# A weight's sign kept as a signed zero that POOL or VectorE makes, and a new fixed order of instructions

## The chip, the core and the metric

One core of a Trainium2 chip runs the whole program. The metric is the device time of one execution in microseconds (us). TensorE (PE in the profile) does the matrix products, VectorE (DVE), ScalarE (ACT) and GpSimd (POOL) the elementwise work, SyncE (SP) issues the DMAs.

## The reference

Attention in which a query sees only the keys of its own cluster, and behind it a feed-forward net with a softplus. The weights reach the device as 64-bit floats (a float32 draw times a float64 scale), all other inputs as float32.

```python
q_assign = argmax(einsum(q / |q|, c / |c|))          # 4 x 8 x 768 rows of 64, 16 clusters per head
k_assign = argmax(einsum(k / |k|, c / |c|))
scores = where(q_assign[..., None] == k_assign[..., None, :], q @ k.T / 8, -1e9)
attn = softmax(scores)
x = (attn @ v).transpose(0, 2, 1, 3).reshape(3072, 512)
h = x @ w_in                                          # w_in 512 x 2048
out = (maximum(h, 0) + log1p(exp(-abs(h)))) @ w_out   # w_out 2048 x 512
```

## The kernel before

Every product is made of three float16 products: an operand is split into a high part (a cast) and a low part (the operand minus that cast). There are 192 score tiles of 128 queries by 768 keys, numbered by `t`. For each one TensorE makes the scores into PSUM (line 1021), VectorE takes the negated row maximum `negm` from PSUM (line 1037), ScalarE the exponential (line 1048); the result is split (helpers `cast` at line 539 and `sub` at line 529), transposed by DMA or by TensorE, and multiplied with `v` into `mbank` (lines 1153 to 1159). The first net layer `h` (lines 1236 to 1238) and the second `o` (lines 1319 to 1321) of a stretch of 384 tokens follow among the score tiles of later stretches, so TensorE has products of three stages at once. Where the writer of the program saw a gap on TensorE early on, filler products are issued (line 494).

The order of the work is written out. Each step of each task is a generator that yields operations; the list `SEQUENCE` names them one after the other. An entry is 1000 x choice + task: the task's next operation is issued, and if it can run on several engines the choice says on which (0 the first one named). The planner's costs and biases that stand in the yields (660, 420, `SBIAS`) do not choose anything in this program; the list does. Each engine runs its instructions in the order of the list.

The change is in `prep_weights`. The two weights are loaded in 32 steps of 128 rows by 512 columns of 64-bit words, 16 for `w_in` and 16 for `w_out`, most of them into tiles that later hold other parts of `wo` (so the profile calls the loaded words `wo`, and two `wraw`). `low` and `high` are the two 32-bit words of each number, so reads and writes of them step over every second word. A step does this before: ScalarE makes the magnitude (`AF.Abs` of the high word, scaled, line 663); the low word is shifted right by 29, on VectorE (line 669) or by a scaled `Relu` on ScalarE (line 670); VectorE joins the sign bit of the high word with the shifted low word (line 678), and joins the magnitude, shifted left by 3, into that (line 684). Then `cast` and `sub` split it (lines 539 and 529). Step s+1 waits for the magnitude of step s, and a step from the third on waits for a score tile (`sc`, one per 1.2 steps), so the steps spread over the first 40 or so score tiles. `cast` can run on ScalarE, VectorE or POOL, `sub` on POOL or VectorE.

```python
yield op("ACT", 660, lambda: nc.scalar.activation(mag, val, AF.Abs, scale=sc))
od.set(("wd", step))
yield op(("DVE", "ACT"), (420, 770), (
    lambda: nc.vector.tensor_scalar(low, low, 29, None, ALU.logical_shift_right),
    lambda: nc.scalar.activation(low, top, AF.Relu, bias=down, scale=2.0**-13)), ...)
yield op("DVE", 685, lambda: nc.vector.scalar_tensor_tensor(
    high, high, -0x80000000, low, ALU.bitwise_and, ALU.bitwise_or), shared=True)
yield op("DVE", 685, lambda: nc.vector.scalar_tensor_tensor(
    high, mab, 3, high, ALU.logical_shift_left, ALU.bitwise_or), shared=True)
```

Of the kernel before, what the change touches and what calls it, by code (L numbers as in the profile page):

```python
# [9 lines left out]
F32 = mybir.dt.float32  # L10
I32 = mybir.dt.int32
I64 = mybir.dt.int64
U16 = mybir.dt.uint16
# [24 lines left out]
SLACK = 0  # L38
BIAS = 500
# [366 lines left out]
def tile_cluster_attention__then__softplus_ffn(  # L406
# [91 lines left out]
    def op(eng, ns, emit, **opt):  # L498
        return ("op", eng, ns, emit, opt)
# [915 lines left out]
```

## Time and profile before

| | |
|---|---|
| time, median of 3 runs | 825.93 us (825.83 to 826.98) |
| the profiled execution | 828.08 us, of which the span from the first to the last instruction is 826.3 us |
| TensorE busy | 809.5 us, 98% of the span |
| VectorE busy | 641.5 us, 78% |
| ScalarE busy | 566.6 us, 69% |
| POOL busy | 444.7 us, 54% |
| granted TensorE clock | 0.999 of full |

The shares of the whole span are averages over stages with different limits: up to 200 us VectorE and ScalarE are busy almost all the time, after that TensorE alone. The stage has to be chosen before a row is read, and POOL's and VectorE's rows have to be read together.

### The profile page before, as it was taken

The numbers are of one execution on the slowest core, as the hardware profiler recorded it, in microseconds if no ns is written. First come the engines' busy times: TensorE is split into PE (matmuls) and PEld (weight loads), VectorE is DVE, ScalarE is ACT, GpSimd is POOL, SyncE is SP. The second block draws the span as 40 slices with busy tenths as digits, with TensorE's granted clock in tenths as the row PEclk, the third lists the DMA queues.
The fourth block names the chain that finished last, engine by engine and source line by source line (L and its number), as shares of the span: only waits on it lengthen the run. The fifth ranks groups of instructions, "written<-read, shape, count | busy, mean of one in ns | idle before, by whom it ended". The sixth has DMA issues, their size and how long they took to land.

```text
span 826.3 us, 19518 instructions
## 1 busy us (share of the span) xinstructions
PE 809.5 (98%) x7904; PEld 518.4 (63%) x7904; DVE 641.5 (78%) x1142; ACT 566.6 (69%) x977; POOL 444.7 (54%) x353
## 2 busy tenths in 40 slices
PE   8999989999999999999999999999999999999998
PEld 8888866665666666656665656656666665555553
DVE  8999989998868887779795879878898776632432
ACT  7999998997867768666676658585567665443330
POOL 4226444646775746674567374766575755632220
PEclk9999999999999999999999999999999999999999
DMA  9436999999979999999989979999969966640001
GB/s 330 153 85 160 213 195 232 210 208 180 210 160 193 182 194 198 206 198 206 166 134 181 171 150 193 206 217 176 192 128 181 179 127 105 115 90 13 27 1 39
DMA packets 386315, 134.29 MB, mean 163 GB/s; under 512 B 362672, under 2 KB 379056, under 8 KB 386224
## 3 DMA queue, kind: packets, MB, share of 16 engines
q1 hardware_dynamic: 386224, 133.03, 80.8%
q8 instruction: 62, 1.02, 0.5%
q14 instruction: 29, 0.24, 0.1%
HBM read 35.68 MB, written 6.29 MB: 51 GB/s over the span
## 4 chain that ended last, share of the span: by engine, by line
PE 73%; DVE 9%; ACT 8%; DMA 6%; POOL 3%; issue 2%; SPq 0%; POOLq 0%; DVEq 0%; ACTq 0%
PE s L1021 10%; PE o L1319 9%; PE o L1321 9%; PE o L1320 9%; PE h L1236 8%; PE h L1238 8%; PE h L1237 8%; PE mbank L1159 3%; PE mbank L1157 3%; PE mbank L1158 3%; DMA pt<-phl 2%; DVE negm L1037 2%; ACT p L1048 2%; DVE wo L678 1%; DMA rawq<-in_q_dram 1%
## 5 line engine op out<-in xcount | busy, mean ns | idle before, releaser
L1048 ACT ACTIVATE p<-s,negm 128x768 f32<-128x768 f32 x190 | 170.5, 901 | 95.0 <-DVE negm L1037 77.2
L1037 DVE TENSOR_REDUCE negm<-s 128x1 f32<-128x768 f32 x192 | 181.2, 948 | 35.5 <-PE s L1021 35.0
L529 POOL TENSOR_TENSOR phl<-p,phl 128x768 f16<-128x768 f32 x87 | 148.8, 1717 | 71.3 <-ACT phl L539 45.8
L1236 PE MATMUL h<-xT,wi 128*128 128x384 f16 x512 | 166.7, 326 | 1.4 <-ACT fg L1275 0.5
L1238 PE MATMUL h<-xT,wi 128*128 128x384 f16 x512 | 166.8, 326 | 0.0
L1237 PE MATMUL h<-xT,wi 128*128 128x384 f16 x512 | 166.8, 326 | 0.0
L1021 PE MATMUL s<-kt,qt 128*128 128x384 f16 x768 | 155.8, 326 | 4.2 <-ACT p L1048 2.3
L1321 PE MATMUL o<-wo,gh 128*128 128x512 f16 x384 | 145.5, 379 | 0.0
L1320 PE MATMUL o<-wo,gh 128*128 128x512 f16 x384 | 145.5, 379 | 0.0
L1319 PE MATMUL o<-wo,gh 128*128 128x512 f16 x384 | 145.4, 379 | 0.0
L1285 POOL TENSOR_TENSOR fg<-fg,fa 128x384 f32<-128x384 f32 x63 | 67.4, 1072 | 93.3 <-ACT fa L1281 90.0
L1157 PE MATMUL mbank<-vb,pt 128*128 128x65 f16 x1008 | 108.9, 192 | 3.2 <-DVE fg L1285 1.6
L1158 PE MATMUL mbank<-vb,pt 128*128 128x64 f16 x1008 | 109.0, 192 | 0.0
L1159 PE MATMUL mbank<-vb,pt 128*128 128x65 f16 x1008 | 108.7, 194 | 0.0
L1157 PEld LDWEIGHTS <-pt 128*128 128x128 f16 x1008 | 93.7, 98 | 15.9 <-DMA pt<-phl 3.9
L1021 PEld LDWEIGHTS <-qt 128*128 128x128 f16 x768 | 71.4, 98 | 50.4 <-issue 5.8
L1158 PEld LDWEIGHTS <-pt 128*128 128x128 f16 x1008 | 93.0, 97 | 12.5 <-issue 0.6
L1159 PEld LDWEIGHTS <-pt 128*128 128x128 f16 x1008 | 93.2, 97 | 0.0
L539 ACT CAST phl<-p 128x768 f16<-128x768 f32 x97 | 79.6, 829 | 19.0 <-DMA pt<-phl 12.8
L529 DVE TENSOR_TENSOR phl<-p,phl 128x768 f16<-128x768 f32 x75 | 84.1, 1132 | 8.2 <-ACT phl L539 3.4
L1267 ACT ACTIVATE fa<-h 128x384 f32<-128x384 f32 x78 | 38.1, 489 | 66.5 <-PE h L1238 56.2
L529 POOL TENSOR_TENSOR gh<-fg,gh 128x768 f16<-128x768 f32 x35 | 58.7, 1676 | 25.1 <-ACT gh L539 20.6
(177 smaller groups left out, 1460.0 us busy)
## 6 DMA issues: line engine op xcount, KB each, us to landing
wo<-in_moe_w_in_dram SPq DMA_DIRECT2D x16, 512.0 KB, 6.3
wo<-in_moe_w_out_dram SPq DMA_DIRECT2D x14, 512.0 KB, 4.3
rawk<-in_k_dram SPq DMA_DIRECT2D x16, 384.0 KB, 4.8
rawq<-in_q_dram SPq DMA_DIRECT2D x16, 384.0 KB, 4.2
rawv<-in_v_dram SPq DMA_DIRECT2D x16, 384.0 KB, 4.2
out_dram<-ot SPq DMA_DIRECT2D x24, 256.0 KB, 2.4
pt<-phl SPq DMA_TRANSPOSE x82, 5.9
wraw<-in_moe_w_out_dram SPq DMA_DIRECT2D x2, 512.0 KB, 5.5
```

Of the source, the lines that this page charges most:

```text
L529: [lambda e=e: e.tensor_tensor(dst, a, b, ALU.subtract) for e in (nc.gpsimd, nc.vector)],
L1021: nc.tensor.matmul(st[:, j, :SH], qt[:, s, i], kt[:, s, NT // 2 * j : NT // 2 * (j + 1)], start=(s == 0), stop=(s == 1),)
L1037: yield op("DVE", 950, lambda: nc.vector.tensor_reduce(negm, st[:, :, :SH], AX.XY, ALU.max, negate=True))
L1157: nc.tensor.matmul(av, pt[:, 0, c], vb[:, c, D : 2 * D + 1], start=(c == 0), stop=False)
L1158: nc.tensor.matmul(av[:, :D], pt[:, 0, c], vb[:, c, :D], start=False, stop=False)
L1159: nc.tensor.matmul(av, pt[:, 1, c], vb[:, c, D : 2 * D + 1], start=False, stop=(c == NT - 1))
L1236: nc.tensor.matmul(hp, w[0], x[0], start=(c == 0), stop=False)
L1237: nc.tensor.matmul(hp, w[0], x[1], start=False, stop=False)
L1238: nc.tensor.matmul(hp, w[1], x[0], start=False, stop=(c == NP - 1))
L1319: nc.tensor.matmul(po, g[0], wo[:, f, 0, 0], start=(f == f0), stop=False)
L1320: nc.tensor.matmul(po, g[0], wo[:, f, 0, 1], start=False, stop=False)
L1321: nc.tensor.matmul(po, g[1], wo[:, f, 0, 0], start=False, stop=(f == f0 + NF // 2 - 1))
```

## The change

In a weight step the magnitude becomes `Copy` with a scale (its sign stays, and is shifted out later), which ScalarE, POOL or VectorE may do. The low word is no longer shifted by itself. The high word is multiplied by 0.0 in place, on VectorE or POOL, which leaves a zero with the number's sign; this operation writes what the magnitude reads, so it waits for it. The first join shifts the low word by 29 and joins it with that signed zero; the second is as before. So the step has as many operations as before. The constant `down` and its fill go. In `prep_k` the copy of the high part of a key becomes a `cast` with a choice of engine. The list is another one throughout, of the same length, 3654 entries.

```diff
-        yield op("ACT", 660, lambda: nc.scalar.activation(mag, val, AF.Abs, scale=sc))
+        yield op(
+            ("ACT", "POOL", "DVE"),
+            (686, 640, 420),
+            (
+                lambda: nc.scalar.activation(mag, val, AF.Copy, scale=sc),
+                lambda: nc.gpsimd.tensor_scalar(mag, val, sc, None, ALU.mult),
+                lambda: nc.vector.tensor_scalar(mag, val, sc, None, ALU.mult),
+            ),
+            shared=True,
+            bias=MBIAS,
+        )
         od.set(("wd", step))
         yield op(
-            ("DVE", "ACT"),
-            (420, 770),
-            (
-                lambda: nc.vector.tensor_scalar(low, low, 29, None, ALU.logical_shift_right),
-                lambda: nc.scalar.activation(low, top, AF.Relu, bias=down, scale=2.0**-13),
-            ),
+            ("DVE", "POOL"),
+            (420, 640),
+            [lambda e=e: e.tensor_scalar(val, val, 0.0, None, ALU.mult) for e in (nc.vector, nc.gpsimd)],
             shared=True,
             bias=SBIAS,
         )
         yield op(
             "DVE",
             685,
-            lambda: nc.vector.scalar_tensor_tensor(high, high, -0x80000000, low, ALU.bitwise_and, ALU.bitwise_or),
+            lambda: nc.vector.scalar_tensor_tensor(high, low, 29, high, ALU.logical_shift_right, ALU.bitwise_or),
             shared=True,
         )
...
-            yield op("ACT", 830, lambda: nc.scalar.copy(n2[:, :, :D], n1[:, :, D:]))
+            yield cast(n2[:, :, :D], n1[:, :, D:], NT * P)
```

What the two lists say, read by walking them through the generators: all 32 magnitudes stay on ScalarE, and so do the 12 key copies. The shifts of before stand 19 times on ScalarE and 13 times on VectorE; the multiplications by zero of after stand 18 times on POOL and 14 times on VectorE. TensorE's 969 operations come in the same order but for exchanges among neighbours: 457 keep their place, and none moves by more than 7. From behind the first row maximum (`t` = 0) up to and with the 49th (`t` = 48) these counts differ, among the operations that read and write SBUF alone:

| operation | before | after |
|---|---|---|
| shift, then multiplication by zero | POOL 0, ACT 17 | POOL 16, ACT 0, and one more on VectorE |
| weight `cast` | | 2 fewer on POOL, 2 more on ACT |
| weight `sub` | | 2 more on POOL, 1 fewer on VectorE |
| key `sub` | | 1 more on POOL, 1 fewer on VectorE |
| `cast` of `p` | | 1 more on POOL, 1 fewer on VectorE |
| `sub` of `p` | | 2 fewer on POOL, 2 more on VectorE |

## Rows read from the trace of the kernel before

**Rows 1.** The page: the span, busy time and share of each engine (part 1), and the busy tenths and granted clock in 40 slices of 20.7 us (part 2).

```profile
span 826.3 us, 19518 instructions
...
PE 809.5 (98%) x7904; PEld 518.4 (63%) x7904; DVE 641.5 (78%) x1142; ACT 566.6 (69%) x977; POOL 444.7 (54%) x353
...
DVE  8999989998868887779795879878898776632432
ACT  7999998997867768666676658585567665443330
...
PEclk9999999999999999999999999999999999999999
```

**Rows 2.** Windows: the length of a stretch, then busy us of each engine with the number of its instructions, granted clock, DMA share and GB/s. The first row lasts from the end of the first row maximum to the end of the 49th; the others follow it up to 780 us.

```profile
24.00:181.00 157.00, 148.75 (x1537) 114.75 (x1534) 151.65 (x280) 150.33 (x281) 73.60 (x61) 1.00 0.83 176
...
181.00:240.00 59.00, 58.14 (x583) 35.61 (x582) 47.76 (x87) 41.68 (x70) 37.13 (x27) 1.00 1.00 194
240.00:780.00 540.00, 539.13 (x5177) 327.39 (x5176) 406.75 (x667) 343.54 (x572) 319.11 (x242) 1.00 0.85 160
```

**Rows 3.** Groups of VectorE's instructions in the stretch from 24 to 181 us, by line and shape: count, busy us and mean ns of one, then idle time before them. First the row maximum, which reads PSUM; then those that read and write SBUF alone, down to groups of 0.9 us.

```profile
L1037 DVE TENSOR_REDUCE negm<-s 128x1 f32<-128x768 f32 x48 | 44.6, 945 | 0.8 <-PE s L1021 0.8
L678 DVE SCALAR_TENSOR_TENSOR wo<-wo 128x512 int32<-128x512 int32 x30 | 20.8, 694 | 0.7 <-ACT wo L663 0.3
L684 DVE SCALAR_TENSOR_TENSOR wo<-wi,wo 128x512 int32<-128x512 int32 x16 | 10.8, 679 | 0.0
L684 DVE SCALAR_TENSOR_TENSOR wo<-wo 128x512 int32<-128x512 int32 x14 | 10.3, 740 | 0.0
L529 DVE TENSOR_TENSOR phl<-p,phl 128x768 f16<-128x768 f32 x8 | 8.0, 1013 | 0.1
L669 DVE TENSOR_SCALAR wo<-wo 128x512 int32<-128x512 int32 x12 | 5.1, 422 | 0.0
L1285 DVE TENSOR_TENSOR fg<-fg,fa 128x384 f32<-128x384 f32 x9 | 5.0, 571 | 0.0
L529 DVE TENSOR_TENSOR gh<-fg,gh 128x768 f16<-128x768 f32 x4 | 4.1, 1034 | 0.0
...
L922 DVE SCALAR_TENSOR_TENSOR qn<-rawq,qn 128x768 f16<-128x768 f32 x3 | 2.8, 946 | 0.0
L529 DVE TENSOR_TENSOR wo<-wo 128x512 f16<-128x512 f32 x4 | 2.7, 686 | 1.6 <-POOL wo L539 1.6
L529 DVE TENSOR_TENSOR wi<-wo,wi 128x512 f16<-128x512 f32 x4 | 2.7, 681 | 0.0
L971 DVE TENSOR_SCALAR n<-n 128x96 f16<-128x96 f16 x3 | 2.4, 784 | 0.0
L529 DVE TENSOR_TENSOR vb<-rawv,vb 128x768 f16<-128x768 f32 x2 | 1.9, 952 | 0.0
...
L529 DVE TENSOR_TENSOR xn<-x,xn 128x384 f16<-128x384 f32 x2 | 1.1, 549 | 0.0
...
L922 DVE SCALAR_TENSOR_TENSOR qn<-rawq,qn 128x384 f16<-128x384 f32 x2 | 1.1, 542 | 0.0
...
L529 DVE TENSOR_TENSOR kn<-rawk,kn 128x768 f16<-128x768 f32 x1 | 0.9, 950 | 0.0
```

**Rows 4.** One line's instructions over the whole run: the least, the median and the greatest duration in ns, when the first and the last start. The row maximum; subtractions and casts on POOL and VectorE; VectorE's second join and its small product of line 971; POOL's product of line 977, which works on two sizes.

```profile
L1037 DVE TENSOR_REDUCE negm<-s x192: 915/947/959, 23.0 to 717.3; 128x1 f32<-128x768 f32 x192
...
L529 POOL TENSOR_TENSOR phl<-p,phl x87: 1631/1644/2450, 101.4 to 721.5; 128x768 f16<-128x768 f32 x87
L529 DVE TENSOR_TENSOR phl<-p,phl x75: 939/952/2384, 94.8 to 721.3; 128x768 f16<-128x768 f32 x75
...
L529 POOL TENSOR_TENSOR wi<-wo,wi x12: 1154/1168/1512, 34.3 to 79.7; 128x512 f16<-128x512 f32 x12
...
L529 POOL TENSOR_TENSOR kn<-rawk,kn x6: 1642/1742/2362, 116.2 to 501.2; 128x768 f16<-128x768 f32 x6
...
L539 POOL CAST phl<-p x33: 813/822/1635, 205.3 to 716.5; 128x768 f16<-128x768 f32 x33
...
L539 DVE CAST phl<-p x32: 540/550/1737, 175.1 to 720.8; 128x768 f16<-128x768 f32 x32
...
L539 POOL CAST wi<-wo x5: 647/654/1050, 29.4 to 81.1; 128x512 f16<-128x512 f32 x5
...
L684 DVE SCALAR_TENSOR_TENSOR wo<-wo x14: 676/684/1449, 84.7 to 176.8; 128x512 int32<-128x512 int32 x14
...
L971 DVE TENSOR_SCALAR n<-n x4: 180/759/835, 19.1 to 54.8; 128x96 f16<-128x96 f16 x4
...
L977 POOL TENSOR_TENSOR n<-qn,aq x18: 825/1468/2182, 19.1 to 658.5; 128x768 f16<-128x768 f16 x14, 128x384 f16<-128x384 f16 x4
```

**Rows 5.** The timeline (start and duration in us) around 176 us, one row of POOL's and one of VectorE's.

```profile
175.85 1.88 POOL L529 TENSOR_TENSOR phl<-p,phl 128x768 f16<-128x768 f32 x1 [5.01 <-ACT fg L1275]
...
176.83 1.45 DVE L684 SCALAR_TENSOR_TENSOR wo<-wo 128x512 int32<-128x512 int32 x1
```

**Rows 6.** ScalarE's shift of the low words from 24 to 181 us, as in rows 3.

```profile
L670 ACT ACTIVATE wo<-wo,down 128x512 int32<-128x512 uint16 x17 | 13.1, 780 | 0.0
```

**Rows 7.** Who released TensorE from its waits between 24 and 181 us: us in total, times, longest.

```profile
PE s L1021 <- ACT p L1048: 2.0, 5, 0.6
...
PE h L1236 <- ACT fg L1275: 0.5, 1, 0.5
```

More of the change, by code (lines that the diff above doesn't have):

```diff
@@ L38 @@
 SLACK = 0
+MBIAS = 500
 BIAS = 500
@@ L622, in tile_cluster_attention__then__softplus_ffn @@
     rooms = {}
-    down = cpool.tile([P, 1], F32, name="down")
-    nc.vector.memset(down, 2.0**-14 - 0.5)
     def prep_weights(step: int):
@@ L649, in prep_weights @@
         low, high = words[:, :, 0], words[:, :, 1]
-        top = raw64.bitcast(U16).rearrange("p (e t) -> p e t", t=4)[:, :, 1]
         val = high.bitcast(F32)
```

328 rows, old and new, of the table SEQUENCE are left out of this document.

## The prediction

> **What bounds the kernel now.** I read the page first. TensorE is busy 98% of the span at the full granted clock, so the whole can gain little; but VectorE's and ScalarE's slices show eights and nines for the first ten slices, some 200 us, and sixes and sevens after them [rows 1]. All 32 weight steps lie in that first part, so the windows are cut there. From the end of the first row maximum to the end of the 49th, 24 to 181 us, VectorE is busy 151.65 of 157.0 us, ScalarE 150.33, TensorE 148.75, POOL only 73.60. From 181 to 240 us TensorE has 58.14 of 59, and from 240 to 780 us 539.13 of 540 [rows 2]. So in the first part the elementwise engines set the pace, and behind it TensorE runs without gaps: what the first part gains or loses moves the end by as much, because TensorE has no room in which to make it up.
>
> On this reading POOL has 83 us free in the first part, and ScalarE's work could go there at no cost. Whether it can is seen in the durations. VectorE's row maximum, which reads PSUM, takes 915 to 959 ns in 192 cases, whatever POOL does. VectorE's instructions that work on SBUF alone have a median near their least and a far greater maximum: the subtraction 952 and 2384 ns, the small product of line 971 180 and 835; POOL's have the same tails (1644 and 2450, a cast 654 and 1050) [rows 4]. The timeline shows why: POOL's subtraction runs from 175.85 to 177.73 us, VectorE's join starts at 176.83 and lasts 1.45 us instead of its 0.684, so it does its work when POOL is through [rows 4, 5]. POOL and VectorE's SBUF work take turns.
>
> So the resource to add up is this turn: all of POOL's time plus VectorE's time on SBUF alone. VectorE's groups of that kind in the first part, added down the list from line 678 to the last row: 20.8 + 10.8 + 10.3 + 8.0 + 5.1 + 5.0 + 4.1 + 2.8 + 2.7 + 2.7 + 2.4 + 1.9 + 1.1 + 1.1 + 0.9 = 79.7 us [rows 3]. With POOL's 73.6 that is 153.3 of 157.0 us [rows 2]. Some of it is waiting, counted on both sides: on VectorE 14 x (740 - 684) + 8 x (1013 - 952) + 4 x (1034 - 952) + 3 x (784 - 180) ns = 3.4 us [rows 3, 4]. POOL's own waiting is in the sum too, and VectorE's groups under 0.9 us are not; I let these two cancel. That leaves 149.9 us of work in turn, and 7.1 us of room in 157. POOL looks half idle, yet the turn is 95% full.
>
> The Trainium skill has this as a rule: SBUF — State Buffer, section "SBUF: two separate sides", says that VectorE and GpSimd share a pair of SBUF ports by an exclusive lock held for the whole instruction, by VectorE's two-input and fast one-input SBUF operations, while ScalarE has ports of its own. By that rule the trace agrees (1449 ns for a join of 684 beside POOL), and the rule speaks against this change. Without it, POOL counted as free, the change would come out faster by the price in the first rival.
>
> **The change part by part.** ScalarE's shifts go: in the first part 17 of 0.780 us, 13.1 us [rows 6]. That is 9% of ScalarE's time there, and it used no turn. ScalarE takes two weight casts back.
>
> The multiplications by zero come. No row shows one. On VectorE I take the shift of the low words, 422 ns for the same 128 x 512 words with the same step [rows 3]; there is one more of them than there were shifts, +0.4 us. On POOL the nearest row is its cast of the same words, 654 ns: one input, same count, same step. The bounds are from nothing, if POOL did it in turns that nobody wants, to POOL's two-input subtraction on the same count, 1168 ns [rows 4]. I take 0.654, since it too reads one tensor. 16 of them in the first part: +10.5 us in turn.
>
> The new list moves other work [rows 3, 4]. Two weight casts leave POOL: -1.3. Two weight subtractions go onto POOL and one leaves VectorE: 2 x 1.168 - 0.681 = +1.7. One key subtraction goes from VectorE to POOL: 1.742 - 0.950 = +0.8. One cast of `p` does so: 0.822 - 0.550 = +0.3. Two subtractions of `p` go the other way: 2 x (0.952 - 1.644) = -1.4. The first join costs what it did, since it is the same instruction with two SBUF inputs; the second is untouched. The magnitude stays on ScalarE in all 32 steps, `Copy` for `Abs` with the same shape, so nothing. The key copies stay on ScalarE, nothing. The fill of `down` was one column before the first score tile, nothing.
>
> In sum the turn gets 10.5 + 0.4 - 1.3 + 1.7 + 0.8 + 0.3 - 1.4 = 11.0 us more in the first part, 160.9 us of work for 157.0 us. VectorE's own work does not change by 1 us, and it has 5.4 us idle in the stretch, so a POOL instruction that takes the turn mostly makes VectorE late, and with it the row maxima, the exponentials and TensorE.
>
> The new wait, the zero behind the magnitude, holds the joins of its step. In 19 steps the shift already followed the magnitude on the same engine, 0.78 us behind it, so the chain of a step grows in 13 steps only, by 0.42 to 0.65 us. Behind a waiting zero on VectorE stands the next row maximum in its list; on POOL a subtraction. No load is moved, and TensorE's list keeps its order but for exchanges of up to seven places, so no DMA queue is passed by anything else.
>
> If all the room were used up, the 49th row maximum would end 160.9 - 157.0 = 3.9 us later; if the room of before stays, because it comes from POOL lacking an operand and not from choice, 11.0 us later. Nearer the second: the room is small, VectorE leaves little, and the new pieces are short and each need a turn of their own. ScalarE's relief helps a little the other way. I let a third of the room go: 11.0 - 7.1 / 3 = 8.6 us.
>
> The profiled execution took 828.08 us, 826.3 of span and 1.8 around it; it lies 2.15 us above the median of 825.93. On its scale the forecast is 828.1 + 8.6 = 836.7, on that of the median 825.9 + 8.6 = 834.5 us.
>
> **The rivals.** Faster: ScalarE is the limit of the first part, and the room in the turn takes the zeros. For it speaks ScalarE's 150.33 of 157 [rows 2]. Then TensorE gets back what ScalarE's waits cost it, 2.0 + 0.5 us [rows 7], and the time is 823.4. It decides if the turn holds less than 146 us of work, since only then do 11.0 fit into 157. Against it stands the sum, 149.9. Chance 0.07.
>
> No change: POOL's zeros fall under VectorE's PSUM work, 44.6 us of row maxima and more, and ScalarE's gain pays for the rest. Against it: POOL's 73.6 us already have to fit into the 77 us that VectorE's 79.7 leave. 825.9 within 1.6. Chance 0.06.
>
> Dearer: POOL's multiplication costs what its two-input operations do, or the list, whose TensorE order was barely touched while the engines behind it run otherwise, opens gaps after 181 us where there were 1.7 us in 600 [rows 2]. The first is 16 x (1.168 - 0.654) = 8.2 us more, 842.7. Nothing in the rows speaks for it, and nothing excludes it. Chance 0.10.
>
> **How the numbers follow.** The forecast has 0.77. Its own range is 3.9 to 11.0 us, 829.8 to 836.9. To leave out no more than 2 in 10 the range goes to 829.0 below, short of both the faster and the unchanged case (0.13), and to 841.0 above, which takes in most of the dearer one. A measurement of this kernel can tell about 0.2% from no change, 1.6 us. Faster by more has 0.07; within it 0.06; slower 0.77 + 0.10 = 0.87.
>
> **What the profile of after would show.** If the steps are right: POOL busy up by some 10 us within the first 49 row maxima; ScalarE less than 90% busy there; VectorE still without idle time, its means on SBUF lines (678, 684 and 529 of before) further above their medians; the 49th row maximum ending at 185 to 192 us instead of 181; and from there to the end the same time as before. A zero on POOL at 0.64 to 0.70 us. I am wrong if the 49th row maximum ends at 181 or earlier with POOL that much busier, for then the turn was not full; or if the time is lost after 200 us, for then the new order and not the turn did it; or if the zeros take far from 0.65 us.

## The result, and the profile after

The changed kernel takes 832.62 us (median of 3 runs, 832.55 to 832.81) against 825.93 us (825.83 to 826.98): a ratio of 1.0078, 95% interval 1.0055 to 1.0101. It is slower, and 834.5 us had been forecast. The profiled execution took 832.81 us, of which the span is 831.0 us. It lies 0.2 us above the median of its kernel, while that of before lay 2.15 us above its own; so the medians differ by 6.7 us and the two traces by 4.7 us of span.

The page of the changed kernel, to be laid beside [rows 1]: span, busy time and share of each engine, and the tenths in 40 slices.

```profile
span 831.0 us, 19676 instructions
...
PE 814.4 (98%) x7992; PEld 523.7 (63%) x7992; DVE 653.6 (79%) x1126; ACT 558.5 (67%) x969; POOL 476.0 (57%) x376
...
DVE  8999999999887987889777878887587887743222
ACT  7998789977867668677476555786587565433530
...
PEclk9999999999999999999999999999999999999999
```

POOL has 31 us more and ScalarE 8 us less, as the change has it; but VectorE has 12 us more, and it was given 16 instructions fewer (1126 against 1142). Its nines now reach the tenth slice without a break, and the clock is full throughout. The windows say where the time went; the first lasts again from the end of the first row maximum to the end of the 49th, as in [rows 2]:

```profile
23.80:186.10 162.30, 154.28 (x1602) 119.36 (x1601) 158.31 (x280) 142.20 (x265) 101.30 (x77) 1.00 0.78 173
186.10:250.00 63.90, 63.17 (x646) 39.06 (x645) 57.59 (x97) 48.92 (x82) 35.52 (x28) 1.00 0.87 182
250.00:790.00 540.00, 539.01 (x5168) 327.52 (x5167) 406.25 (x649) 338.54 (x573) 321.66 (x251) 1.00 0.79 159
```

The first part took 162.3 instead of 157.0 us, and its end lies 5.1 us later. Behind it nothing more is lost: TensorE is busy 63.17 of 63.9 us and 539.01 of 540 us, as before. So the question is what made the first part 5.3 us longer. VectorE is busy 158.31 us in it instead of 151.65 (+6.7) and idle 4.0 instead of 5.35 (-1.4), which is the 5.3. VectorE's groups in that stretch, with count, busy us, mean ns of one, and idle time before them, answer to [rows 3]:

```profile
L1042 DVE TENSOR_REDUCE negm<-s 128x1 f32<-128x768 f32 x48 | 44.8, 947 | 0.0
L683 DVE SCALAR_TENSOR_TENSOR wo<-wo 128x512 int32<-128x512 int32 x30 | 24.0, 810 | 2.4 <-POOL wo L676 2.2
...
L530 DVE TENSOR_TENSOR phl<-p,phl 128x768 f16<-128x768 f32 x10 | 10.2, 1026 | 0.0
...
L1290 DVE TENSOR_TENSOR fg<-fg,fa 128x384 f32<-128x384 f32 x10 | 7.6, 767 | 0.0
L676 DVE TENSOR_SCALAR wo<-wo 128x512 f32<-128x512 f32 x13 | 6.8, 520 | 0.2
```

The row maximum, which reads PSUM, is unchanged (947 against 945 ns). What works on SBUF is dearer by the piece: the first join 810 against 694 ns, 30 x 0.116 = 3.5 us; the product of line 1290 767 against 571, 10 x 0.196 = 2.0 us; the multiplication by zero 520 against the shift's 422, 13 x 0.098 = 1.3 us. These three come to 6.8 us; what the list moves to VectorE and away from it cancels within 1 us, and other groups go both ways (the second join of line 689 on `wo` alone has 686 ns, against 740 before). The first two are of the same kind and size as before, the third takes what the shift took when nothing hinders it (its median stands below), so what was added is waiting that the trace counts as busy. Beside it, VectorE's longest waits from 10 to 210 us are now for POOL's zeros (us in total, times, longest):

```profile
DVE wo L683 <- POOL wo L676: 2.2, 3, 1.5
DVE wraw L683 <- POOL wraw L676: 1.4, 1, 1.4
```

And the zeros on POOL are no 0.65-us instructions. First the group in the stretch, then least, median and greatest duration in ns of all on POOL and on VectorE:

```profile
L676 POOL TENSOR_SCALAR wo<-wo 128x512 f32<-128x512 f32 x16 | 28.5, 1779 | 5.4 <-ACT wi L665 2.4 <-ACT wo L665 2.1 <-POOL n L982 0.9
...
L676 POOL TENSOR_SCALAR wo<-wo x17: 1562/1589/2399, 17.5 to 178.5; 128x512 f32<-128x512 f32 x17
...
L676 DVE TENSOR_SCALAR wo<-wo x13: 419/428/894, 26.3 to 148.9; 128x512 f32<-128x512 f32 x13
```

The median is 1.589 us, 2.4 times the price that the forecast took and above the upper bound of 1.168 too. VectorE's was taken rightly (428 against 422 ns). If POOL's whole time were in turn with VectorE, as the forecast had it, its 27.7 us more in the first part (101.30 - 73.60) could not have cost 5.3 us only. So the forecast came near with a term that was far off, and the experiments ask why.

### The profile page after: what moved, and what is told of

It is laid out like the page before. It is cut to its first block, busy times and chain, and to the rows that moved or that the text cites. A ratio compares the mean times of both kernels' runs of the same rounds, so it can differ in the third digit from the quotient of the medians.

```text
span 831.0 us, 19676 instructions
## 1 busy us (share of the span) xinstructions
PE 814.4 (98%) x7992; PEld 523.7 (63%) x7992; DVE 653.6 (79%) x1126; ACT 558.5 (67%) x969; POOL 476.0 (57%) x376
## 4 chain that ended last, share of the span: by engine, by line
PE 73%; DVE 13%; ACT 4%; issue 4%; POOL 3%; DMA 3%; SPq 0%; POOLq 0%; DVEq 0%; ACTq 0%
PE s L1026 10%; PE o L1326 9%; PE o L1324 9%; PE o L1325 9%; PE h L1241 8%; PE h L1242 8%; PE h L1243 8%; PE mbank L1164 3%; PE mbank L1162 3%; PE mbank L1163 3%; DVE negm L1042 3%; DVE wo L683 2%; POOL wo L676 2%; DVE wo L689 1%; DMA pt<-phl 1%
## 5 line engine op out<-in xcount | busy, mean ns | idle before, releaser
L530 POOL TENSOR_TENSOR phl<-p,phl 128x768 f16<-128x768 f32 x81 | 138.3, 1711 | 65.6 <-DVE phl L540 35.6
L1290 POOL TENSOR_TENSOR fg<-fg,fa 128x384 f32<-128x384 f32 x64 | 71.6, 1122 | 78.8 <-ACT fa L1286 78.5
L530 DVE TENSOR_TENSOR phl<-p,phl 128x768 f16<-128x768 f32 x81 | 92.9, 1152 | 5.7 <-ACT phl L540 3.3
L1272 ACT ACTIVATE fa<-h 128x384 f32<-128x384 f32 x82 | 40.3, 491 | 80.7 <-PE h L1243 63.4
L540 ACT CAST phl<-p 128x768 f16<-128x768 f32 x92 | 75.3, 828 | 3.6 <-DMA pt<-phl 2.5
L1285 ACT ACTIVATE fa<-fa 128x384 f32<-128x384 f32 x128 | 65.8, 522 | 10.6 <-DVE fa L1268 10.5
```

The costliest lines, as they stand in the source:

```text
L530: [lambda e=e: e.tensor_tensor(dst, a, b, ALU.subtract) for e in (nc.gpsimd, nc.vector)],
```

## The experiments

The theory to be tested was the forecast's: POOL's new time is taken from VectorE, instruction by instruction. Its rivals: the new list did it; the new wait (magnitude, zero, join) lengthens each step's chain; POOL's instructions are dear by their length and not by the turn. The kernels were run against the kernel before, on the same chip; the ratio is the comparison, since medians of before lay between 827.14 and 827.42 us in these runs. "Stretch" is the time from the end of the first to the end of the 49th row maximum in the one profiled execution. It can mislead by 2 or 3 us: the profiled executions of before, e2, e3 and e6 lie 2.1 to 3.3 us above the medians of their kernels, the others within 1.1 us, and the start of the stretch lies between 23.8 and 26.1 us.

| kernel | list | zero or shift is made by | median us | ratio (95%) | stretch us | VectorE busy, idle |
|---|---|---|---|---|---|---|
| before | old | ScalarE (shift), VectorE | 825.93 | 1 | 157.0 | 151.65, 5.35 |
| e3 | old | ScalarE, VectorE | 827.22 | 0.9997 (0.9985 to 1.0009) | 157.9 | 151.26, 6.6 |
| e1 | old | POOL, VectorE | 846.80 | 1.0231 (1.0214 to 1.0248) | 172.3 | 162.51, 9.8 |
| e2 | new | ScalarE (shift), VectorE | 825.18 | 0.9971 (0.9960 to 0.9983) | 154.4 | 151.39, 3.0 |
| e5b | new | POOL by a copy, VectorE | 831.05 | 1.0048 (1.0029 to 1.0066) | 158.4 | 155.55, 2.8 |
| after | new | POOL, VectorE | 832.62 | 1.0078 (1.0055 to 1.0101) | 162.3 | 158.31, 4.0 |
| e9 | new | POOL, two inputs, VectorE | 836.71 | 1.0107 (1.0082 to 1.0132) | 163.9 | 161.09, 2.8 |
| e6 | new | VectorE | 835.64 | 1.0108 (1.0093 to 1.0124) | 167.3 | 159.92, 7.4 |
| e8 | new | POOL, twice each, VectorE | 862.00 | 1.0419 (1.0405 to 1.0433) | 187.9 | 166.44, 21.5 |

Idle is the stretch less the busy time. The granted clock of TensorE in the stretch is 0.95 in e8, 0.98 in e1 and e6, and 0.99 or 1.00 in the others; what that adds to the losses was not taken apart. Two more kernels, e4 and e7, time single instructions. A first form of e5b, which copied the high words onto themselves, gave no time.

### The operations or the list: e1 and e2

The two kernels exchange their lists. With the old list under the new code, the 19 shifts of ScalarE become zeros on POOL in the same places (e1); with the new list under the old code, POOL's zeros become shifts on ScalarE (e2).

```diff
 SEQUENCE = [   # e1: code of after, list of before
-    0, 0, 0, 0, 0, 0, 0, 0, 0, 0, 1, 2, 4, 0, 1, 0, 6, 468, 469, 1001, 0, 468, 0, 0, 3, 1, 468, 2004, 1, 0, 468, 1,
+    0, 0, 0, 0, 1, 0, 0, 2, 0, 0, 0, 0, 0, 4, 1, 0, 468, 1001, 0, 1, 0, 468, 0, 0, 469, 0, 468, 3, 1, 1468, 0, 1,
...
 SEQUENCE = [   # e2: code of before, list of after
-    0, 0, 0, 0, 1, 0, 0, 2, 0, 0, 0, 0, 0, 4, 1, 0, 468, 1001, 0, 1, 0, 468, 0, 0, 469, 0, 468, 3, 1, 1468, 0, 1,
+    0, 0, 0, 0, 0, 0, 0, 0, 0, 0, 1, 2, 4, 0, 1, 0, 6, 468, 469, 1001, 0, 468, 0, 0, 3, 1, 468, 2004, 1, 0, 468, 1,
...
```

> The new operations under the list of before: the 19 shifts that stood on ScalarE become multiplications by zero on POOL at the same places, the other 13 stay on VectorE. Theory one (POOL's zeros make the loss: 1.59 us each on POOL, part of it in turn with VectorE): 831 to 838 us. Theory two (the new list, not searched, makes the loss; the operations cost nothing): 824 to 827 us.

> The operations of before under the new list: the 18 zeros that stood on POOL become shifts on ScalarE (0.78 us each). Theory one (POOL's zeros): 825 to 828 us, as before or a little above. Theory two (the list): 831 to 834 us, as after.

The windows of e1, then its wait row; behind it the windows of e2:

```profile
24.80:197.10 172.30, 156.17 (x1613) 120.39 (x1610) 162.51 (x281) 140.89 (x263) 103.50 (x78) 0.98 0.72 162
```

```profile
DVE wo L683 <- POOL wo L676: 6.4, 5, 2.3
```

```profile
24.50:178.90 154.40, 147.25 (x1517) 113.96 (x1515) 151.39 (x281) 150.28 (x282) 72.59 (x60) 1.00 0.84 180
```

The operations alone cost 2.3%, three times the loss of the whole change and more than either range that was expected of e1; the list alone gains 0.3%. So the list did no harm; it takes back two thirds of what the operations cost (2.3% against 0.8%), and under the old operations it makes a kernel that beats both. The 10.0 us between the stretches of e1 and of after are VectorE's again: 4.2 of busy time and 5.8 of idle time, most of the latter in the wait for the zeros (6.4 against 2.2 us on the tile `wo`).

### The longer chain, or POOL: e3

e1 again, but the 19 zeros are made by ScalarE, which in the forecast's account uses none of VectorE's turn. Its product has no sign here, so these weights lose theirs.

```diff
-            ("DVE", "POOL"),
+            ("DVE", "ACT"),
             (420, 640),
-            [lambda e=e: e.tensor_scalar(val, val, 0.0, None, ALU.mult) for e in (nc.vector, nc.gpsimd)],
+            (
+                lambda: nc.vector.tensor_scalar(val, val, 0.0, None, ALU.mult),
+                lambda: nc.scalar.activation(val, val, AF.Copy, scale=0.0),
+            ),
```

> As the first, but the 19 multiplications by zero that went to POOL are made by ScalarE (Copy with scale 0.0), so POOL gets none. Theory one: 824 to 827 us, since the shift on ScalarE took 0.78 us and this should take about 0.7. If instead the new chain of a step (zero behind magnitude, both joins) costs something by itself, 828 or more, whatever engine makes the zero.

The windows of e3:

```profile
26.10:184.00 157.90, 148.85 (x1538) 114.81 (x1535) 151.26 (x280) 149.03 (x281) 73.83 (x61) 1.00 0.83 174
```

No change (0.9997), and VectorE as busy as before. The zero waits for the magnitude in all 32 steps here as well, and the join for both. So neither the new wait nor the new join costs anything that can be measured: the whole 2.3% of e1 comes with POOL. Two limits: in 19 steps the zero stands behind the magnitude on ScalarE, as the shift did, so the wait is new in the 13 steps on VectorE only; and a chain that goes over POOL, with its longer zero, is not in this run but in e1.

### What one POOL instruction costs VectorE: e4 and e7

Both compute nothing of the reference. They issue POOL instructions on 128 x 512 words with the step of 2, alone and beside VectorE's. In e4 the instructions came in another order than written, so it says nothing of the turn; only POOL's durations are taken from it. e7 has the written order: four POOL instructions, and beside them 14 joins, or 20 multiplications by zero, or 10 row maxima of PSUM on VectorE.

```diff
+    for d, n in ((None, 0), (d_join, 14), (d_mult, 20), (d_max, 10)):
+        for g in KINDS:       # multiply, the same without a step, cast, copy, two inputs, subtract
+            meet()            # both engines start together
+            for _ in range(4):
+                g()
+            for _ in range(n):
+                d()
```

> A kernel that computes nothing of the reference: four POOL instructions of each of five kinds on 128 x 512 words (multiplication by zero with a step of two words, the same without a step, a cast, a copy, a two-input multiplication), first with VectorE idle, then beside 8 joins, 12 multiplications by zero or 8 maxima from PSUM on VectorE. If POOL's instruction holds the turn from its start to its end: beside 8 joins (0.68 us each) the stretch takes the sum, 4 x 1.59 + 8 x 0.68 = 11.8 us for the strided multiplication, and joins of up to 2.2 us are seen. If it holds it for a part, some 0.5 us of 1.59: about 4 x 0.5 + 5.4 = 7.4 us, joins of at most 1.2 us. Beside maxima from PSUM nothing gets longer. Alone, the strided multiplication takes 1.57 us if that is its own price, and about 0.65 us if the 1.59 of the full kernel is waiting.

> The measurement beside idle and busy VectorE again, now with the instructions in the written order, longer rows on VectorE (14 joins, 20 multiplications, 10 maxima from PSUM) and POOL's subtraction as a sixth kind; it computes nothing of the reference. If POOL's multiplication (1.53 us alone) holds the turn throughout, VectorE's 14 joins last 9.5 + 4 x 1.53 = 15.6 us beside four of them; if for a part of some 0.45 us, 11.3 us. Beside maxima from PSUM no instruction gets longer.

Least, median and greatest duration of POOL's instructions in e4, the multiplication, the cast and the two-input multiplication:

```profile
L59 POOL TENSOR_SCALAR wg<-wg x16: 1528/1532/1552, 5.1 to 126.1; 128x512 f32<-128x512 f32 x16
L68 POOL CAST gout<-wg x16: 621/628/634, 18.7 to 129.8; 128x512 f16<-128x512 f32 x16
...
L74 POOL TENSOR_TENSOR wg<-wg,gz x16: 1482/1487/1488, 50.7 to 138.0; 128x512 f32<-128x512 f32 x16
```

The multiplication by a constant has 1.53 us, as long as a multiplication of two tensors and 2.4 times the cast, the forecast's nearest row. In e7 the four that POOL makes while VectorE has nothing to do have it too (first row below), so it is neither waiting nor the turn that makes it long. Nor is it the step of two words: without it the multiplication takes 1.49 us alone. e7, groups by window: the multiplication alone; beside the joins first POOL's multiplication, then its cast, then its two-input multiplication; then VectorE's multiplications beside POOL's multiplication and beside its cast, and its PSUM maxima beside POOL's multiplication.

```profile
L60 POOL TENSOR_SCALAR wg<-wg 128x512 f32<-128x512 f32 x4 | 6.1, 1531 | 0.4 <-DMA wg<-in_moe_w_in_dram 0.2
...
L78 DVE SCALAR_TENSOR_TENSOR wd<-wd 128x512 int32<-128x512 int32 x14 | 11.1, 791 | 0.4
L60 POOL TENSOR_SCALAR wg<-wg 128x512 f32<-128x512 f32 x4 | 6.6, 1645 | 0.2
...
L69 POOL CAST gout<-wg 128x512 f16<-128x512 f32 x4 | 3.6, 888 | 0.2
...
L78 DVE SCALAR_TENSOR_TENSOR wd<-wd 128x512 int32<-128x512 int32 x14 | 14.5, 1036 | 0.4
L75 POOL TENSOR_TENSOR wg<-wg,gz 128x512 f32<-128x512 f32 x4 | 6.9, 1732 | 0.2
...
L81 DVE TENSOR_SCALAR wd<-wd 128x512 f32<-128x512 f32 x20 | 11.7, 586 | 0.7
...
L81 DVE TENSOR_SCALAR wd<-wd 128x512 f32<-128x512 f32 x20 | 9.9, 497 | 0.7
...
L84 DVE TENSOR_REDUCE mx<-st 128x1 f32<-128x512 f32 x10 | 6.9, 690 | 0.3
```

The joins' row is the same beside the cast as beside the multiplication: 14 in 11.1 us, mean 791 ns. Their median beside the multiplication, 694 ns, is near their least, so it is taken for that of a join which nothing hinders; the row of 20 multiplications is read in the same way:

```profile
L78 DVE SCALAR_TENSOR_TENSOR wd<-wd x15: 681/694/1146, 37.3 to 49.2; 128x512 int32<-128x512 int32 x15
...
L81 DVE TENSOR_SCALAR wd<-wd x20: 418/429/878, 114.7 to 126.6; 128x512 f32<-128x512 f32 x20
...
L84 DVE TENSOR_REDUCE mx<-st x10: 682/691/692, 189.9 to 196.4; 128x1 f32<-128x512 f32 x10
```

So each POOL multiplication costs the joins 14 x (791 - 694) / 4 ns = 0.34 us, and so does a cast that is less than half as long. A two-input POOL instruction costs them 14 x (1036 - 694) / 4 = 1.20 us of its 1.49. VectorE's own multiplication loses more to POOL's, 20 x (586 - 429) / 4 = 0.79 us each, but no more to POOL's cast than the joins do, 20 x (497 - 429) / 4 = 0.34. The timeline shows the difference: within one multiplication on POOL (from 116.70 us, 1.60 us long) two of VectorE's are longer than 0.43 us (from 116.94 us 0.74, from 117.71 us 0.87), while of the joins beside one only one is. The ten PSUM maxima lose nothing: they take 682 to 692 ns each. Had POOL's multiplication held the turn for its whole length, the 14 joins would have taken 14 x 0.694 and most of 4 x 1.53, some 15 us. Against a join, one-input POOL instructions hold the turn briefly, whatever their length; against VectorE's one-input multiplication the long one costs twice what the short one does; two-input ones hold the turn for most of their length.

The kernel itself shows it too. In the timeline of after, a multiplication by zero starts on POOL at 52.71 us and lasts till 54.29; a join that starts at 53.41 is not held up at all:

```profile
52.71 1.58 POOL L676 TENSOR_SCALAR wo<-wo 128x512 f32<-128x512 f32 x1
...
53.41 0.68 DVE L689 SCALAR_TENSOR_TENSOR wo<-wi,wo 128x512 int32<-128x512 int32 x1
...
163.62 2.40 POOL L676 TENSOR_SCALAR wo<-wo 128x512 f32<-128x512 f32 x1 [0.41 <-ACT wo L665]
166.03 0.99 POOL L1290 TENSOR_TENSOR fg<-fg,fa 128x384 f32<-128x384 f32 x1
166.05 1.52 DVE L683 SCALAR_TENSOR_TENSOR wo<-wo 128x512 int32<-128x512 int32 x1 [1.54 <-POOL wo L676]
```

The last three rows are the case that costs. VectorE stands 1.54 us for a zero; when it ends, POOL's next instruction, of two inputs, starts 0.02 us ahead of the released join, and the join of 0.688 us (median) takes 1.52. Two more joins come right behind a zero and beside POOL's next two-input instruction:

```profile
74.06 1.67 DVE L683 SCALAR_TENSOR_TENSOR wo<-wo 128x512 int32<-128x512 int32 x1
...
97.95 1.64 DVE L683 SCALAR_TENSOR_TENSOR wo<-wo 128x512 int32<-128x512 int32 x1 [0.30 <-POOL wo L676]
```

The three take 1.67 + 1.64 + 1.52 - 3 x 0.688 = 2.8 us more than unhindered joins, most of what the first joins lost (3.5 us).

### The forecast's own assumption, a POOL zero as short as a cast: e5b

POOL writes the zero by a copy instead of a multiplication; these weights lose their sign.

```diff
+    zero = cpool.tile([P, 1], F32, name="zero")
+    nc.vector.memset(zero, 0.0)
...
-            [lambda e=e: e.tensor_scalar(val, val, 0.0, None, ALU.mult) for e in (nc.vector, nc.gpsimd)],
+            (
+                lambda: nc.vector.tensor_scalar(val, val, 0.0, None, ALU.mult),
+                lambda: nc.gpsimd.tensor_copy(val, zero.to_broadcast([P, WC])),
+            ),
```

> The changed kernel and its list, but the 18 operations on POOL copy a plain zero into the high words instead of multiplying them by zero (these weights lose their sign). A copy took 0.63 us alone and made a join beside it 0.31 us longer, the multiplication 1.53 us and the same 0.31. If the forecast's own term is right for a piece of 0.65 us (the whole of it in turn), 830 to 837 us. If a one-input operation costs VectorE its 0.31 to 0.45 us whatever its length, the waits inside VectorE's instructions stay near the 12 us of after and only the idle time before the joins goes: 829 to 832 us. If the length of 1.53 us is what costs, 825 to 828 us.

The windows; the groups of the copy (from 24 to 181 us), of the first join and of line 1295 (1290 of after); and the same place of the timeline as above:

```profile
24.80:183.20 158.40, 153.84 (x1603) 118.92 (x1602) 155.55 (x282) 142.37 (x266) 85.69 (x76) 1.00 0.80 177
```

```profile
L680 POOL COPY wo<-zero 128x512 f32<-128x512 f32 x16 | 12.3, 769 | 5.8 <-ACT wo L667 2.5 <-ACT wi L667 2.3 <-POOL n L987 0.9
...
L688 DVE SCALAR_TENSOR_TENSOR wo<-wo 128x512 int32<-128x512 int32 x30 | 20.9, 709 | 0.6 <-POOL wo L680 0.6
...
L1295 DVE TENSOR_TENSOR fg<-fg,fa 128x384 f32<-128x384 f32 x10 | 7.6, 764 | 0.0
```

```profile
161.87 1.43 POOL L680 COPY wo<-zero 128x512 f32<-128x512 f32 x1 [0.39 <-ACT wo L667]
163.34 0.69 DVE L688 SCALAR_TENSOR_TENSOR wo<-wo 128x512 int32<-128x512 int32 x1 [0.56 <-POOL wo L680]
...
164.30 1.46 POOL L1295 TENSOR_TENSOR fg<-fg,fa 128x384 f32<-128x384 f32 x1 [0.99 <-ACT fa L1291]
...
164.82 1.49 DVE L694 SCALAR_TENSOR_TENSOR wo<-wo 128x512 int32<-128x512 int32 x1
```

The loss is 3.6 us (831.05 against 827.42) and not the 8.6 that the forecast gave to pieces of this length. The time lies in two of the three expected ranges, so it does not decide between them by itself. Against e2, which has the same list and no zero on POOL, the ratio is up by 0.0077, some 6.4 us or 0.40 us for each of the 16 copies of the first part (0.29 to 0.51 by the two intervals): near the 0.34 that e7 measured, and not their whole length of 0.63 us.

Against after, the stretch is 3.9 us shorter: 2.8 of busy and 1.1 of idle time. The first joins have 20.9 instead of 24.0 us, more than the 2.8; other groups go both ways. In the timeline the join waits 0.56 instead of 1.54 us and then runs unhindered, for POOL's next instruction lacks its operand until 164.30 us. (That instruction then meets the second join, which takes 1.49 us, so here only the shorter wait is gained.) So by the rows the multiplication's extra length is paid at the join behind it: by waiting for it, and by meeting POOL's next instruction. As a time this is not shown: 1.0 of the 3.9 us comes from a stretch that starts later, the spans of the two executions differ by 1.9 us, the ratios by 0.3%, and the intervals of e5b and after overlap. What stays with the short piece is the turn and what POOL does later in another place: line 1295's product has 764 ns here too, mostly from one that takes 1.83 us beside POOL's two-input product of line 987.

### Away from POOL altogether: e6

```diff
-            [lambda e=e: e.tensor_scalar(val, val, 0.0, None, ALU.mult) for e in (nc.vector, nc.gpsimd)],
+            [lambda: nc.vector.tensor_scalar(val, val, 0.0, None, ALU.mult)] * 2,
```

> The changed kernel and its list, but the 18 zeros of POOL are made by VectorE (0.43 us each, 7.7 us in all, in front of the joins where they are needed at once). If the loss is what VectorE has to do or wait for, this lies near after, since VectorE gets 7 us of work in the first part and loses some 10 us of waiting there: 829 to 834 us. If the loss is POOL's own lateness (its later subtractions), 825 to 829 us.

The windows of e6:

```profile
24.50:191.80 167.30, 157.45 (x1603) 121.76 (x1602) 159.92 (x298) 142.60 (x266) 74.82 (x60) 0.98 0.73 168
```

1.0108, above the expected range, and a stretch 5.0 us longer than that of after, in an execution 3.1 us above the median of e6. VectorE has 16 zeros more, 16 x 0.428 = 6.8 us of own work, and loses less in turn, so it ends at 159.92 us busy; but it is idle for 7.4, most of it before row maxima whose scores TensorE had not made (the first row of its waits from 10 to 215 us):

```profile
DVE negm L1042 <- PE s L1026: 5.4, 5, 1.6
```

Why TensorE was late there was not taken apart. By the medians POOL's zeros cost a little less than VectorE's own would (0.8% against 1.1%, intervals that just overlap): they are dear, but VectorE is no better place for them. The best one is ScalarE's (e2, e3).

### More of POOL's time: e8 and e9

e8 issues each POOL zero twice. e9 makes it by a product of two tensors, which in e7 held the turn for most of its length.

```diff
-            [lambda e=e: e.tensor_scalar(val, val, 0.0, None, ALU.mult) for e in (nc.vector, nc.gpsimd)],
+            (
+                lambda: nc.vector.tensor_scalar(val, val, 0.0, None, ALU.mult),
+                lambda: [nc.gpsimd.tensor_scalar(val, val, 0.0, None, ALU.mult) for _ in range(2)],   # e8
+                lambda: nc.gpsimd.tensor_tensor(val, val, zero.to_broadcast([P, WC]), ALU.mult),      # e9
+            ),
```

> The changed kernel and its list, each of POOL's 18 multiplications issued twice in a row: 28 us more on POOL. If POOL's time in turn makes the loss, it grows by as much again as a zero of 1.53 us costs over none, 7 us or more: 839 to 855 us. If the loss comes from the order or from the chain of a step, 833 to 837 us.

> The changed kernel and its list, but the 18 operations on POOL multiply the high words by a tile of zeros (two inputs) instead of by a constant. In order and alone such an operation took 1.48 us, as long as the one-input one (1.53), but made a join beside it 1.17 us longer instead of 0.31. If what VectorE waits for is the part held, it loses 16 x 0.86 = 14 us more in the first 49 score tiles at most: 838 to 848 us. If it is POOL's time that costs, 831 to 834 us, as after.

The windows of e8 and its wait row; behind them the windows of e9 and the group of its zeros (from 24 to 181 us):

```profile
25.10:213.00 187.90, 162.46 (x1627) 125.22 (x1626) 166.44 (x282) 142.88 (x266) 128.47 (x92) 0.95 0.65 149
```

```profile
DVE wo L686 <- POOL wo L678: 16.3, 11, 3.2
```

```profile
24.90:188.80 163.90, 155.94 (x1603) 120.59 (x1601) 161.09 (x281) 142.21 (x266) 92.24 (x76) 0.99 0.78 171
```

```profile
L680 POOL TENSOR_TENSOR wo<-wo,zero 128x512 f32<-128x512 f32 x16 | 19.4, 1210 | 6.0 <-ACT wi L667 2.4 <-ACT wo L667 2.0 <-POOL n L987 0.9
```

e8's time, 862.00 us, lies above both expected ranges, and that of e9, 836.71 us, between its two. Twice the zeros put 27.2 us more on POOL and make the stretch 25.6 us longer, 8.1 of it VectorE's busy time and 17.5 its idle time. Most is the wait of the joins for the zero, 16.3 us in 11 cases. This looks like the forecast's picture, in which all of POOL's time counts, but it is a different thing: a second zero of 1.6 us stands in the chain of its step, and VectorE waits at the join. By e5b and e8 the length of a POOL zero is cheap where the join comes later than it ends, and is paid in full where VectorE is at the join already.

In e9 the second input is one column of zeros, and the product takes 1.21 us on average, not the 1.48 that was expected. So e9 takes POOL 9 us less than after does, and yet VectorE is 2.8 us busier and 1.2 us less idle. That is the two prices seen apart: a shorter instruction that holds the turn for longer. As a time it settles nothing, since its interval overlaps with that of after.

## Why the prediction came out as it did

**Where the first part's time goes, and that the rest adds nothing: right.** The 49th row maximum was to end at 185 to 192 us; it ends at 186.0. After it, TensorE runs without gaps as before. ScalarE is below 90% (142.20 of 162.3), and the first join's mean is further above its median (810 and 688 ns, before 694 and 682), as forecast; the second join on `wo` did not follow (686 ns, before 740).

**That POOL is no free place, and that ScalarE's relief does not pay for it: right.** e3 against e1 shows both at once: the zeros cost nothing on ScalarE and 2.3% on POOL, although ScalarE is relieved there. (What ScalarE's relief is worth where POOL costs nothing, no run shows.) The rule of the Trainium skill (SBUF — State Buffer, section "SBUF: two separate sides") pointed the right way. But it states that whichever of POOL's instruction and VectorE's two-input one starts first keeps the pair of ports for its whole length and blocks the other fully, and for one-input instructions of POOL the measurement differs: a join loses 0.34 us to a multiplication of 1.53 us, and one of 0.68 us runs in the midst of one (52.71 and 53.41 us). For two-input ones it comes near, 1.20 of 1.49 us.

**The price of POOL's zero: wrong.** 0.654 us was taken from the cast, with 1.168 as the upper bound; it is 1.53 alone and 1.589 in the kernel. The row was chosen because it also reads one tensor. What was wanted was a row that does arithmetic, and before had none on POOL with one input and that size; the subtraction, which was kept as the upper bound, was the nearer neighbour, and even it was too low. POOL's busy time in the first part is up by 27.7 us and not by some 10. The prediction itself had named zeros that take far from 0.65 us as a sign of being wrong, and that sign came. The rival "dearer" was nearer to this price with 1.168, and its time, 842.7, still did not come; the next step says why. The Trainium skill (GPSIMD Engine Reference, section "Engine selection") says that GpSimd works on one input at roughly line rate; the cast's 0.63 us may pass for that, the multiplication's 1.53 us for as many words does not, and the measurement decides.

**That all of POOL's time is in turn with VectorE's SBUF work: wrong for one-input instructions.** The rows that showed the turn were a subtraction's [rows 5], and it is right for those; it was carried over to casts and to the new operation. The account of 149.9 us of work in a turn of 157 counts too much, and its 7.1 us of room were not a room. (One sentence on the rows does not hold: line 971's median, 759 ns, is not near its least, 180. The trace has its three instructions of the first part beside POOL's product of line 977, so the waiting counted there stands.)

**Why it still came near: luck.** The two errors offset each other. With 0.654 us and the whole of it in turn, the 16 zeros had 10.5 us. Measured against e2, which has the same list, they cost 1.07% (1.0078 less 0.9971), some 8.8 us. With what e7 measured, the turn makes 16 x 0.34 to 16 x 0.79 of that, 5.4 to 12.6 us, depending on what VectorE does beside them. What is not the turn was in no term: the joins that wait for a zero of 1.6 us and then meet POOL's next instruction, which the step on the new wait had put down as a chain longer by 0.42 to 0.65 us. The forecast's 0.65-us piece was tested as such (e5b) and cost 3.6 us, just under the 3.9 to 11.0 of its own range. And where the forecast took off 2.4 us for room, the list gave back 2.0.

**What the list moves, 0.1 us in the forecast's sum (11.0 - 10.5 - 0.4): mis-sized.** It gains 2.0 us under the old operations (825.18 against 827.14, e2), and with the new ones makes up two thirds of their loss (2.3% in e1, 0.8% in after).

**Open.** Why POOL's multiplication costs a join 0.34 us once and VectorE's one-input multiplications 0.79 us in two pieces: that was measured, not explained. How the 6.7 us split between the turn and the waits: the rows name the places, but no time tells after from e5b or e9. And which of the list's moves gains what was not taken apart.

## What to carry to other kernels

Work given to POOL is paid in two coins: what its instruction holds of the turn with VectorE, which was most of a two-input one (1.20 of 1.49 us) and, against a join, little of a one-input one (0.34 of 1.53 us), and its length, which is paid only if somebody waits for it. Ask of each moved instruction who stands behind it in VectorE's order, and what POOL does next at that moment, for it will be ahead. And price an operation by a row that does the same kind of work, not by one with the same operands: a cast of 0.63 us said nothing of a multiplication of 1.53.

## What was not expected of the hardware

- POOL's multiplication of one tensor by a constant takes 1.53 us on 128 x 512 float32, as long as that of two tensors (1.49) and 2.4 times as long as a cast or a copy of the same words (0.63).
- A one-input POOL instruction delays VectorE's two-input joins by 0.34 us whether it lasts 0.63 or 1.53 us; a two-input one delays it by 1.20 of its 1.49 us.
- VectorE's one-input float32 multiplication loses more beside POOL's multiplication (0.79 us each, spread over two of them) than its two-input join does; beside POOL's cast it loses the same 0.34 us.
